# Read-out products moved into the last slots, a new tail order, outputs sent by quarters, and the last tile in column halves

## Chip, cores and metric

One core of one Trainium2 chip. The metric is the device time of one execution in microseconds (us), median of several runs. A profile's span, from first to last instruction, is about 1.8 us shorter than the time of the same run (210.28 against 212.04 for the kernel before).

## The reference, cut to what matters

```python
B, H, S, Ns, D = 8, 8, 512, 32, 64
xread = softmax(x @ state^T / 8) @ state           # per batch and head: 512 rows
sread = softmax(state @ x^T / 8) @ x               # 32 "read-out" rows
rows  = concat(xread, sread)                       # 8 batches of 544 rows of H*D = 512
out   = gelu(rows @ w_in) @ w_out                  # 512 -> 2048 -> 512, fp32 out: 4352 x 512
```

## The kernel before

Batches run one after another. In a batch, eight slots p = 0 to 7 each compute two 128-row blocks of the first layer (`M`, tile `hp`, GELU by ScalarE into `g`) beside one product of the second layer of the batch before. From the third batch on, the second layer is a seven-product (Strassen) scheme: products M1 to M7 of sums of quarters of `g` (`gsum`, VectorE) with sums of quarters of `w_out`; their results (`xp`, PSUM) are combined by adds into four quarters of the output. With rows in an upper and a lower half and columns in a left and a right one: M5 gives the upper right, M2 the lower left, M3, M6 and M1 the lower right, M1 and M7 the upper left. The 256 read-out rows of all batches go through the same scheme at the end (`R`, tiles `rp`, `osb`).

```python
def c22(b):                                     # after M2
    xs[b, "v"] = c_tile("v")
    nc.gpsimd.tensor_tensor(out=xs[b, "v"], in0=xs[b, "q"], in1=o[:, :, :NH], op=ALU.subtract)
    nc.vector.tensor_tensor(out=o[:, :, NH:], in0=xs[b, 3], in1=xs[b, "v"], op=ALU.add)
    x_out(b, 1)                                 # lower half of the rows, 512 KB
...
def X7_split(b):                                # last product of the last batch, two tiles
    for j in range(2):
        ps = xs[b, "x", j]
        x_mm(ps, xs[b, "g7"], w_sum["7"], False, (j,))
        nc.vector.tensor_tensor(out=o[:, j, :NH], in0=ps[:, 0, :], in1=xs[b, "u"][:, j, :], op=ALU.add)
        eng = nc.scalar if j else nc.sync
        eng.dma_start(out=rows[:, j, :NH], in_=o[:, j, :NH])     # 128 KB each
...
# the tail, after the last batch's slots
r_sums(); g_sum(b, "5"); X(b, "4"); g_sum(b, "1"); R("3"); R("4"); g_sum(b, "2"); X(b, "5")
nc.sync.dma_start(...)                          # upper right, 256 KB
R("5"); X1_split(b); g_sum(b, "7"); R("1"); X(b, "2"); R("2"); R("6"); R("7"); X7_split(b)
```

The softmax here doesn't subtract the row's maximum and nothing guards it: scores larger than these inputs give would overflow.

Of the kernel before, what the change touches and what calls it, by code (L numbers as in the profile page):

```python
# [12 lines left out]
ALU = mybir.AluOpType  # L13
# [4 lines left out]
def kernel(  # L18
# [8 lines left out]
    nc = tc.nc  # L27
# [471 lines left out]
    def mm2(b, q, j):  # L499
        if q == 0:  # L500
            ops[b, j] = otile([128, d_model], "op")
        ps = ops[b, j]
        for m in range(4 * q, 4 * q + 4):
            nc.tensor.matmul(  # L504
                ps,
                lhsT=gs[b][:, m, j * 128:(j + 1) * 128],
                rhs=w_out_bf[:, m, :],
                start=(m == 0),
                stop=(m == MC - 1),
            )  # L510
        if q == 3:
            rows = out_rows(b, j)
            h = d_model // 2 if j == SJ - 1 and b > 0 else d_model
            evac(ps, [(rows[:, n:n + h], slice(0, 128), n, n + h) for n in range(0, d_model, h)])

    def mm1_sr(m):
        hp = ps_f.tile([128, B * NS], FP32, name="hps", tag="f")
# [37 lines left out]
    def w_sums(i):  # L555
# [7 lines left out]
        )[i])  # L563

    xs = {}
    G_SUMS = {
        "1": ((0, 0), (1, 1), ALU.add),
        "2": ((1, 0), (1, 1), ALU.add),
# [26 lines left out]
    def c_tile(name):  # L595
        return cpool.tile([128, 2, NH], FP32, name=name, tag=name)

    def x_out(b, h):
        rows = out[b * SB:b * SB + S, :].rearrange("(p j) n -> p j n", j=SJ)
        nc.sync.dma_start(out=rows[:, 2 * h:2 * h + 2, :], in_=xs[b, "o", h])  # L600

    def c22(b):
        xs[b, "v"] = c_tile("v")
# [7 lines left out]
    def X(b, name):  # L611
        bank = {"3": 0, "4": 1, "5": 0, "2": 1, "1": 2, "6": 3, "7": 2}[name]
        first = name in "3416"
        if first:
            xs[b, bank] = otile([128, 2, NH], "xp", bank)
        ps = xs[b, bank]
        lhs = {"3": (0, 0), "4": (1, 1)}.get(name)
        lhs = xs[b, "g" + name] if lhs is None else g_q(b, *lhs)
        rhs = {"5": w_q[1][1], "2": w_q[0][0]}.get(name)
        rhs = w_sum[name] if rhs is None else rhs  # L620
        x_mm(ps, lhs, rhs, first)
        if name == "3":
            xs[b, "s3"] = c_tile("s3")
            nc.scalar.copy(out=xs[b, "s3"], in_=ps)
            for h in range(2):
                xs[b, "o", h] = hpool.tile([128, 2, d_model], FP32, name="oh", tag=f"oh{h}")
        elif name == "4":
            xs[b, "s34"] = c_tile("s34")
            nc.vector.tensor_tensor(out=xs[b, "s34"], in0=ps, in1=xs[b, "s3"], op=ALU.add)  # L629
        elif name == "5":  # L630
            o = xs[b, "o", 0][:, :, NH:]
            nc.scalar.copy(out=o, in_=ps)  # L632
            xs[b, "u"] = c_tile("u")
            nc.gpsimd.tensor_tensor(out=xs[b, "u"], in0=xs[b, "s34"], in1=o, op=ALU.subtract)  # L634
        elif name == "2":
            nc.scalar.copy(out=xs[b, "o", 1][:, :, :NH], in_=ps)  # L636
            c22(b)
        elif name == "1":
            xs[b, "q"] = c_tile("q")
            nc.vector.tensor_tensor(out=xs[b, "q"], in0=ps, in1=xs[b, "s34"], op=ALU.add)  # L640
        elif name == "7":
            nc.vector.tensor_tensor(
                out=xs[b, "o", 0][:, :, :NH], in0=ps, in1=xs[b, "u"], op=ALU.add
            )
            x_out(b, 0)

    def X1_split(b):
        xs[b, "q"] = c_tile("q")
        for j in range(2):
            ps = xs[b, "x", j] = otile([128, 1, NH], "xp", 2 - 2 * j)  # L650
            x_mm(ps, xs[b, "g1"], w_sum["1"], True, (j,))
            nc.vector.tensor_tensor(
                out=xs[b, "q"][:, j, :], in0=ps[:, 0, :], in1=xs[b, "s34"][:, j, :], op=ALU.add
            )

    def X7_split(b):
        rows = out[b * SB:b * SB + S, :].rearrange("(p j) n -> p j n", j=SJ)
        o = xs[b, "o", 0]
        for j in range(2):
            ps = xs[b, "x", j]  # L660
            x_mm(ps, xs[b, "g7"], w_sum["7"], False, (j,))
            nc.vector.tensor_tensor(
                out=o[:, j, :NH], in0=ps[:, 0, :], in1=xs[b, "u"][:, j, :], op=ALU.add
            )
            eng = nc.scalar if j else nc.sync
            eng.dma_start(out=rows[:, j, :NH], in_=o[:, j, :NH])

    rs = {}

    def r_q(h, k):  # L670
        return g_sr[:, MH * k:MH * k + MH, 128 * h:128 * h + 128]

    def r_sums():
        pair = [att.tile([128, 2, MH, 128], BF16, name="rs", tag="xT") for _ in range(2)]
        one = att.tile([128, MH, 128], BF16, name="rs1", tag="AT")
        homes = [pair[0][:, 0], pair[0][:, 1], pair[1][:, 0], pair[1][:, 1], one]
        for name, t in zip("51267", homes):
            (h0, k0), (h1, k1), op = G_SUMS[name]
            nc.vector.tensor_tensor(out=t, in0=r_q(h0, k0), in1=r_q(h1, k1), op=op)
            rs["g" + name] = t  # L680

    def r_out(h):
        nc.sync.dma_start(
# [4 lines left out]
    def R(name):  # L688
        def c_new(n):
            rs[n] = cpool.tile([128, NH], FP32, name="r_" + n, tag="r_" + n)  # L690
            return rs[n]

        bank = {"3": 0, "4": 1, "5": 0, "2": 1, "1": 2, "6": 3, "7": 2}[name]
        first = name in "3416"
        if first:
            rs[bank] = ftile([128, NH], "rp")
        ps = rs[bank]
        lhs = {"3": (0, 0), "4": (1, 1)}.get(name)
        lhs = rs["g" + name] if lhs is None else r_q(*lhs)
        rhs = {"5": w_q[1][1], "2": w_q[0][0]}.get(name)  # L700
        rhs = w_sum[name] if rhs is None else rhs
        for m in range(MH):
            nc.tensor.matmul(  # L703
                ps,
                lhsT=lhs[:, m, :],
                rhs=rhs[:, m, :],
                start=(first and m == 0),
                stop=(m == MH - 1),
                skip_group_check=True,
            )  # L710
        add, sub = ALU.add, ALU.subtract
        if name == "3":
            nc.scalar.copy(out=c_new("s3"), in_=ps)
            for h in range(2):
                rs["o", h] = opool.tile([128, d_model], FP32, name="osb", tag="osb")
        elif name == "4":
            nc.vector.tensor_tensor(out=c_new("s34"), in0=ps, in1=rs["s3"], op=add)
        elif name == "5":
            o = rs["o", 0][:, NH:]
            nc.scalar.copy(out=o, in_=ps)  # L720
            nc.gpsimd.tensor_tensor(out=c_new("u"), in0=rs["s34"], in1=o, op=sub)
        elif name == "1":
            nc.vector.tensor_tensor(out=c_new("q"), in0=ps, in1=rs["s34"], op=add)
        elif name == "2":
            o = rs["o", 1][:, :NH]
            nc.scalar.copy(out=o, in_=ps)
            nc.gpsimd.tensor_tensor(out=c_new("v"), in0=rs["q"], in1=o, op=sub)
        elif name == "6":
            nc.vector.tensor_tensor(out=rs["o", 1][:, NH:], in0=ps, in1=rs["v"], op=add)
            r_out(1)  # L730
        elif name == "7":
            nc.vector.tensor_tensor(out=rs["o", 0][:, :NH], in0=ps, in1=rs["u"], op=add)
            r_out(0)
# [126 lines left out]
    u = 17  # L860
# [24 lines left out]
    for b in range(2, B):  # L885
        nb = b + 1
        for p in range(8):
# [7 lines left out]
                xtr_dma(nb + 1)  # L895
            if p == 5 and nb < B:
                atr_dma(nb)
            if p == 3:
                srt(b)
            M(k, k + 1)  # L900
            if b == 2:
                for _ in range(2 if p < 4 else 1):
# [3 lines left out]
            elif p < 5:  # L906
# [2 lines left out]
                X(b - 1, "45127"[p])  # L909
                if p < 3:  # L910
                    g_sum(b - 1, "127"[p])
            if nb == B and 3 <= p < 7:
                for m in range(4 * p - 12, 4 * p - 8):
                    mm1_sr(m)
            if p == 1:
                sread(b)
                sread_out(b)
            if p == 0 and b + 3 < B:
                nc.gpsimd.tensor_copy(out=hold, in_=gs[b][:, 0, 0:1])  # L919
                load_x(b + 3)  # L920
# [2 lines left out]
                rearr(nb + 1)  # L923
            if p == 2 and nb + 1 < B:
                rearr_ones(nb + 1)
            if p == 5:
                g_sum(b, "6")
                if nb < B:
                    p_run(nb, (0, 1), ((0, 1), (3, 2)))
# [4 lines left out]
                    p_run(nb, (2, 3), ((1, 2), None))  # L934
                X(b, "6")
    b = B - 1
    r_sums()
    g_sum(b, "5")
    X(b, "4")
    g_sum(b, "1")  # L940
    R("3")
    R("4")
    g_sum(b, "2")
    X(b, "5")
    nc.sync.dma_start(
        out=out[b * SB:b * SB + S, :].rearrange("(p j) n -> p j n", j=SJ)[:, 0:2, NH:],
        in_=xs[b, "o", 0][:, :, NH:],
    )
    R("5")
    X1_split(b)  # L950
    g_sum(b, "7")
    R("1")
    X(b, "2")
    R("2")
    R("6")
    R("7")
    X7_split(b)


# [28 lines left out]
```

## Time and profile before

| | before |
|---|---|
| time, median (range), 4 runs | 212.66 us (212.36 to 212.92) |
| span of the profiled run | 210.28 us |
| PE busy | 200.7 us, 95% |
| first matmul of the second batch | 36.80 us |
| last matmul ends | 204.98 us |
| last output lands | 208.47 us |

### The profile page before, as it was taken

The page shows a single profiled execution, that of the slowest core. Times are in us where ns is not written, and L with a number is a line of the kernel's source. Part 1 is how long each engine was busy: PE and PEld are TensorE (multiplying, and loading weights), DVE is VectorE, ACT ScalarE, POOL GpSimd, SP SyncE. Part 2 cuts the span into 40 slices and gives each one's busy share as a digit, 9 for nine tenths or more (in the row PEclk, how much of TensorE's full clock was granted, in tenths as well). Part 3 has the DMA queues.
Part 4 walks back from the last instruction along what each step waited for, and adds up shares of the span by engine and source line. Part 5 has one row for each costly group of instructions (what it writes and reads, how often), then busy time and mean ns, then how long its engine had stood idle before and what let it go on. Part 6 is the DMA issues. An engine that isn't in the chain of part 4 may idle for free.

```text
span 210.3 us, 4666 instructions
## 1 busy us (share of the span) xinstructions
PE 200.7 (95%) x1955; PEld 130.9 (62%) x1963; DVE 134.5 (64%) x213; ACT 132.9 (63%) x240; POOL 65.9 (31%) x73
## 2 busy tenths in 40 slices
PE   7899999998999999999999999999999999999990
PEld 6645444453454577756775677567766777788880
DVE  1835675738829559984899558855885552357530
ACT  3864855679794779557956596678758455860110
POOL 8964301573270025700576007300220022000330
PEclk9999999999999999999999999999999999999997
DMA  6999999699275809355873910250016001300115
GB/s 200 187 172 204 206 194 193 141 203 174 45 100 124 228 0 128 76 199 54 113 90 131 193 29 3 86 165 3 2 58 194 3 0 59 143 0 0 53 64 187
DMA packets 37861, 23.14 MB, mean 110 GB/s; under 512 B 21712, under 2 KB 35280, under 8 KB 37840
## 3 DMA queue, kind: packets, MB, share of 16 engines
q0 software_dynamic: 13936, 8.10, 28.3%
q1 hardware_dynamic: 23216, 14.29, 27.2%
q10 hardware_dynamic: 688, 0.46, 0.7%
q8 instruction: 15, 0.25, 0.5%
q14 instruction: 6, 0.05, 0.1%
HBM read 17.30 MB, written 8.91 MB: 125 GB/s over the span
## 4 chain that ended last, share of the span: by engine, by line
PE 75%; DVE 11%; POOL 4%; DMA 3%; ACT 2%; issue 1%; POOLq 0%; DVEq 0%; ACTq 0%
PE xp L586 27%; PE hp L478 21%; PE op L504 9%; DVE gsum L580 5%; PE p_ps L415 4%; PE hps L519 3%; PE op L532 3%; DMA AT<-a 3%; PE rp L703 3%; DVE a L347 2%; POOL w_in_bf L105 2%; DVE cs L344 1%; PE sr L378 1%; PE pt L324 1%; POOL sbd L95 1%
## 5 line engine op out<-in xcount | busy, mean ns | idle before, releaser
L485 ACT ACTIVATE g<-hp 128x512 bf16<-128x512 f32 x124 | 67.6, 603 | 31.3 <-PE hp L478 26.0
L478 PE MATMUL hp<-AT,P 128*128 128x512 bf16 x248 | 64.2, 380 | 0.7 <-DVE XSR L405 0.4
L586 PEld LDWEIGHTS <-gsum 128*128 128x128 bf16 x480 | 46.5, 98 | 12.0 <-issue 2.1
L580 DVE TENSOR_TENSOR gsum<-g 128x2048 bf16<-128x2048 bf16 x30 | 39.4, 1327 | 0.0
L478 PEld LDWEIGHTS <-P 128*128 128x128 bf16 x248 | 22.1, 98 | 21.7 <-issue 4.0
L586 PE MATMUL xp<-ws,gsum 128*128 128x256 bf16 x288 | 34.4, 273 | 0.0
L427 DVE CAST P<-p_ps 128x512 bf16<-128x512 f32 x31 | 20.0, 683 | 18.1 <-PE p_ps L415 18.1
L634 POOL TENSOR_TENSOR u<-s,oh 128x512 f32<-128x512 f32 x6 | 7.6, 1266 | 66.8 <-ACT oh L632 66.8
L504 PE MATMUL op<-w_out_bf,g 128*128 128x512 bf16 x90 | 23.0, 379 | 0.3
L586 PE MATMUL xp<-ws,g 128*128 128x256 bf16 x192 | 22.9, 273 | 0.0
L586 PE MATMUL xp<-w_out_bf,gsum 128*128 128x256 bf16 x192 | 22.9, 273 | 0.0
L586 PEld LDWEIGHTS <-g 128*128 128x128 bf16 x192 | 18.8, 98 | 4.3
L426 ACT CAST P<-p_ps 128x512 bf16<-128x512 f32 x31 | 17.0, 604 | 6.8 <-PE p_ps L415 6.8
L218 POOL COPY x<-xb 128x1024 bf16<-128x1024 bf16 x12 | 12.6, 1081 | 11.7 <-DMA xb<-in_x_dram 11.7
L504 PEld LDWEIGHTS <-g 128*128 128x128 bf16 x96 | 9.1, 98 | 11.5 <-issue 1.1
L228 POOL COPY xo<-xb 128x1024 bf16<-128x1024 bf16 x12 | 14.5, 1240 | 1.3 <-PE sr L378 1.3
L347 DVE TENSOR_TENSOR a<-e,ics 128x512 bf16<-128x512 bf16 x14 | 13.9, 995 | 0.5
L605 POOL TENSOR_TENSOR v<-q,oh 128x512 f32<-128x512 f32 x6 | 7.6, 1274 | 15.1 <-ACT oh L636 15.1
L629 DVE TENSOR_TENSOR s<-xp,s 128x512 f32<-128x512 f32 x6 | 4.1, 692 | 12.8 <-PE xp L586 12.8
L415 PE MATMUL p_ps<-w_in_bf,sbd 64*32 64x512 bf16 x248 | 11.5, 382 | 0.8 <-ACT g L485 0.7
L344 DVE TENSOR_REDUCE cs<-e 128x16 f32<-128x512 bf16 x14 | 9.5, 676 | 3.8 <-ACT e L331 3.8
L919 POOL COPY hold<-g 128x1 bf16<-128x1 bf16 x3 | 1.0, 330 | 31.5 <-ACT g L485 31.5
(103 smaller groups left out, 214.9 us busy)
## 6 DMA issues: line engine op xcount, KB each, us to landing
out_dram<-oh SPq DMA_DIRECT2D x11, 512.0 KB, 2.9
xb<-in_x_dram POOLq DMA_DIRECT2D x7, 512.0 KB, 6.8
out_dram<-osb SPq DMA_DIRECT2D x9, 256.0 KB, 3.3
w_out_bf<-in_moe_w_out_dram POOLq DMA_DIRECT2D x4, 512.0 KB, 12.5
w_in_bf<-in_moe_w_in_dram POOLq DMA_DIRECT2D x6, 256.0 KB, 11.5
x0f<-in_x_dram SPq DMA_DIRECT2D x3, 256.0 KB, 4.1
w_in_bf<-in_moe_w_in_dram POOLq DMA_DIRECT2D x4, 128.0 KB, 4.3
x0f<-in_x_dram ACTq DMA_DIRECT2D x1, 256.0 KB, 4.6
```

The lines of the kernel that those rows point to most:

```text
L218: nc.gpsimd.tensor_copy(out=A.x4[:, :, :, 64 * t:64 * t + 64].rearrange("p j c d -> p c j d"), in_=src[:, t],)
L228: eng.tensor_copy(out=A.xo[:, :, :, 2 + 64 * t:66 + 64 * t].rearrange("p j c d -> p c j d"), in_=src[:, t],)
L344: nc.vector.reduce_sum(out=cs, in_=e4, axis=AX.X)
L347: nc.vector.tensor_tensor(out=A.a[:, :, hs].rearrange("p g (c n) -> p g c n", n=NS), in0=e4, in1=ics[:, :, :].to_broadcast((128, G, 2, NS) ...
L415: nc.tensor.matmul(ps[t][32 * c:32 * c + 32, :], lhsT=sbd[64 * t:64 * t + 64, b, c, 32 * t:32 * t + 32], rhs=w_in_bf[64 * t:64 * t + 64, c ...
L426: nc.scalar.copy(out=dst[:, 0, :], in_=ps[0])
L427: nc.vector.tensor_copy(out=dst[:, 1, :], in_=ps[1])
L478: nc.tensor.matmul(hp, lhsT=Ps[b][:, t, m * 128:(m + 1) * 128], rhs=atts[b].AT[:, :, t, :], start=(t == 0), stop=(t == 1),)
L485: nc.scalar.activation(out=gs[b][:, m, :], in_=hp, func=AF.Gelu)
L504: nc.tensor.matmul(ps, lhsT=gs[b][:, m, j * 128:(j + 1) * 128], rhs=w_out_bf[:, m, :], start=(m == 0), stop=(m == MC - 1),)
L580: nc.vector.tensor_tensor(out=t, in0=g_q(b, h0, k0), in1=g_q(b, h1, k1), op=op)
L586: nc.tensor.matmul(ps[:, j - js[0], :], lhsT=lhs[:, m, 128 * j:128 * j + 128], rhs=rhs[:, m, :], start=(first and j == js[0] and m == 0), ...
```

## The change

Its intent: let the read-out results leave earlier, so that the end has fewer outputs to drain; send each quarter when it is ready; make the last piece small. "48 transfers" counts the transfers issued by SyncE and ScalarE (42 before).

```diff
@@ mm2: first batches' outputs
-            h = d_model // 2 if j == SJ - 1 and b > 0 else d_model
-            evac(ps, [(rows[:, n:n + h], slice(0, 128), n, n + h) for n in range(0, d_model, h)])
+            evac(ps, [(rows, slice(0, 128), 0, d_model)])
@@ X: M5 and M7 of every batch but the last
+            x_out(b, 0, right)
...
-            x_out(b, 0)
+            x_out(b, 0, left)
@@ L1, L7: last batch (L4, L5, L5_u, L2 likewise; u and v on VectorE, no longer on GpSimd)
+        rows_out(1, both, right, nc.sync)
...
+        for j, pieces in ((0, ((0, NH),)), (1, ((0, h), (h, NH)))):
+            for n0, n1 in pieces:
+                # 8 matmuls into ps[:, 0, n0:n1], one VectorE add, one transfer
+                eng = nc.scalar if j and n0 else nc.sync
+                rows_out(0, slice(j, j + 1), slice(n0, n1), eng)
@@ last batch's attention read, one batch earlier (srt likewise, in slot 7)
+            if p == 4 and nb == B - 1:
+                sread(nb)
+                sread_out(nb)
@@ last batch's slots (nb == B)
-            if nb == B and 3 <= p < 7:
-                for m in range(4 * p - 12, 4 * p - 8):
+            if nb == B and p < 4:
+                for m in range(4 * p, 4 * p + 4):
                     mm1_sr(m)
+            if nb == B:
+                if p == 4:
+                    r_homes()
+                    r_sum("5")
+                    r_sum("2")
+                if p == 5:
+                    g_sum(b, "6")
+                    R("3")
+                    r_sum("1")
+                    R("4")
+                    r_sum("6")
+                    r_sum("7")
+                if p == 6:
+                    R("5")
+                    X(b, "3")
+                    R("2")
+                    R("1")
+                if p == 7:
+                    R("6")
+                    X(b, "6")
+                continue
@@ tail
-    (the order shown above)
+    for name in "521":
+        g_sum(b, name)
+    L4()
+    g_sum(b, "7")
+    L5()
+    L5_u()
+    L2()
+    R("7")
+    L1()
+    L7()
```

More of the change, by code (lines that the diff above doesn't have):

```diff
@@ L565 @@
     xs = {}
+    left, right = slice(0, NH), slice(NH, d_model)
     G_SUMS = {
@@ L596, in c_tile, with x_out @@
         return cpool.tile([128, 2, NH], FP32, name=name, tag=name)
-    def x_out(b, h):
+    def x_out(b, h, ns=slice(None)):
         rows = out[b * SB:b * SB + S, :].rearrange("(p j) n -> p j n", j=SJ)
-        nc.sync.dma_start(out=rows[:, 2 * h:2 * h + 2, :], in_=xs[b, "o", h])
+        nc.sync.dma_start(out=rows[:, 2 * h:2 * h + 2, ns], in_=xs[b, "o", h][:, :, ns])
     def c22(b):
@@ L644, in X, with rows_out, L4, L5 @@
             )
-            x_out(b, 0)
-    def X1_split(b):
-        xs[b, "q"] = c_tile("q")
+            x_out(b, 0, left)
+    def rows_out(h, js, ns, eng):
+        b = B - 1
+        rows = out[b * SB:b * SB + S, :].rearrange("(p j) n -> p j n", j=SJ)
+        eng.dma_start(
+            out=rows[:, 2 * h + js.start:2 * h + js.stop, ns], in_=xs[b, "o", h][:, js, ns]
+        )
+    both = slice(0, 2)
+    def L4():
+        b = B - 1
+        ps = xs[b, 1] = otile([128, 2, NH], "xp", 1)
+        x_mm(ps, g_q(b, 1, 1), w_sum["4"], True)
+        xs[b, "s34"] = c_tile("s34")
+        nc.vector.tensor_tensor(out=xs[b, "s34"], in0=ps, in1=xs[b, "s3"], op=ALU.add)
+        xs[b, "y"] = c_tile("q")
+        nc.vector.tensor_tensor(out=xs[b, "y"], in0=xs[b, 3], in1=xs[b, "s34"], op=ALU.add)
+    def L5():
+        b = B - 1
+        x_mm(xs[b, 0], xs[b, "g5"], w_q[1][1], False)
+        nc.scalar.copy(out=xs[b, "o", 0][:, :, right], in_=xs[b, 0])
+        rows_out(0, both, right, nc.sync)
+    def L5_u():
+        b = B - 1
+        xs[b, "u"] = c_tile("u")
+        nc.vector.tensor_tensor(
+            out=xs[b, "u"], in0=xs[b, "s34"], in1=xs[b, "o", 0][:, :, right], op=ALU.subtract
+        )
+    def L2():
+        b = B - 1
+        x_mm(xs[b, 1], xs[b, "g2"], w_q[0][0], False)
+        c21 = xs[b, "o", 1][:, :, left]
+        nc.scalar.copy(out=c21, in_=xs[b, 1])
+        rows_out(1, both, left, nc.sync)
+        xs[b, "v"] = c_tile("v")
+        nc.vector.tensor_tensor(out=xs[b, "v"], in0=xs[b, "y"], in1=c21, op=ALU.subtract)
+    def L1():
+        b = B - 1
         for j in range(2):
@@ L652, in X1_split, with L7 @@
             nc.vector.tensor_tensor(
-                out=xs[b, "q"][:, j, :], in0=ps[:, 0, :], in1=xs[b, "s34"][:, j, :], op=ALU.add
-            )
-    def X7_split(b):
-        rows = out[b * SB:b * SB + S, :].rearrange("(p j) n -> p j n", j=SJ)
+                out=xs[b, "o", 1][:, j, right],
+                in0=ps[:, 0, :],
+                in1=xs[b, "v"][:, j, :],
+                op=ALU.add,
+            )
+        rows_out(1, both, right, nc.sync)
+    def L7():
+        b = B - 1
         o = xs[b, "o", 0]
-        for j in range(2):
+        h = NH // 2
+        for j, pieces in ((0, ((0, NH),)), (1, ((0, h), (h, NH)))):
             ps = xs[b, "x", j]
-            x_mm(ps, xs[b, "g7"], w_sum["7"], False, (j,))
-            nc.vector.tensor_tensor(
-                out=o[:, j, :NH], in0=ps[:, 0, :], in1=xs[b, "u"][:, j, :], op=ALU.add
-            )
-            eng = nc.scalar if j else nc.sync
-            eng.dma_start(out=rows[:, j, :NH], in_=o[:, j, :NH])
+            for n0, n1 in pieces:
+                for m in range(MH):
+                    nc.tensor.matmul(
+                        ps[:, 0, n0:n1],
+                        lhsT=xs[b, "g7"][:, m, 128 * j:128 * j + 128],
+                        rhs=w_sum["7"][:, m, n0:n1],
+                        start=False,
+                        stop=(m == MH - 1),
+                        skip_group_check=True,
+                    )
+                nc.vector.tensor_tensor(
+                    out=o[:, j, n0:n1],
+                    in0=ps[:, 0, n0:n1],
+                    in1=xs[b, "u"][:, j, n0:n1],
+                    op=ALU.add,
+                )
+                eng = nc.scalar if j and n0 else nc.sync
+                rows_out(0, slice(j, j + 1), slice(n0, n1), eng)
     rs = {}
@@ L671, in r_q, with r_homes @@
         return g_sr[:, MH * k:MH * k + MH, 128 * h:128 * h + 128]
-    def r_sums():
+    def r_homes():
         pair = [att.tile([128, 2, MH, 128], BF16, name="rs", tag="xT") for _ in range(2)]
@@ L676, in r_sums, with r_sum @@
         homes = [pair[0][:, 0], pair[0][:, 1], pair[1][:, 0], pair[1][:, 1], one]
-        for name, t in zip("51267", homes):
-            (h0, k0), (h1, k1), op = G_SUMS[name]
-            nc.vector.tensor_tensor(out=t, in0=r_q(h0, k0), in1=r_q(h1, k1), op=op)
-            rs["g" + name] = t
+        rs["homes"] = dict(zip("51267", homes))
+    def r_sum(name):
+        t = rs["g" + name] = rs["homes"][name]
+        (h0, k0), (h1, k1), op = G_SUMS[name]
+        nc.vector.tensor_tensor(out=t, in0=r_q(h0, k0), in1=r_q(h1, k1), op=op)
     def r_out(h):
@@ L695, in R @@
         if first:
-            rs[bank] = ftile([128, NH], "rp")
+            home = {"3": 1, "4": 2, "6": 2}
+            rs[bank] = otile([128, NH], "rp", home[name]) if name in home else ftile([128, NH], "rp")
         ps = rs[bank]
@@ L720, in R @@
             nc.scalar.copy(out=o, in_=ps)
-            nc.gpsimd.tensor_tensor(out=c_new("u"), in0=rs["s34"], in1=o, op=sub)
+            nc.vector.tensor_tensor(out=c_new("u"), in0=rs["s34"], in1=o, op=sub)
         elif name == "1":
             nc.vector.tensor_tensor(out=c_new("q"), in0=ps, in1=rs["s34"], op=add)
+            nc.vector.tensor_tensor(
+                out=c_new("v"), in0=rs["q"], in1=rs["o", 1][:, :NH], op=sub
+            )
         elif name == "2":
@@ L726, in R @@
             nc.scalar.copy(out=o, in_=ps)
-            nc.gpsimd.tensor_tensor(out=c_new("v"), in0=rs["q"], in1=o, op=sub)
         elif name == "6":
@@ L897 @@
                 atr_dma(nb)
-            if p == 3:
+            if p == 3 and nb < B:
                 srt(b)
+            if p == 7 and nb == B - 1:
+                srt(nb)
             M(k, k + 1)
@@ L911 @@
                     g_sum(b - 1, "127"[p])
-            if nb == B and 3 <= p < 7:
-                for m in range(4 * p - 12, 4 * p - 8):
+            if nb == B and p < 4:
+                for m in range(4 * p, 4 * p + 4):
                     mm1_sr(m)
-            if p == 1:
+            if p == 1 and nb < B:
                 sread(b)
                 sread_out(b)
+            if p == 4 and nb == B - 1:
+                sread(nb)
+                sread_out(nb)
             if p == 0 and b + 3 < B:
@@ L936 @@
     b = B - 1
-    r_sums()
-    g_sum(b, "5")
-    X(b, "4")
-    g_sum(b, "1")
-    R("3")
-    R("4")
-    g_sum(b, "2")
-    X(b, "5")
-    nc.sync.dma_start(
-        out=out[b * SB:b * SB + S, :].rearrange("(p j) n -> p j n", j=SJ)[:, 0:2, NH:],
-        in_=xs[b, "o", 0][:, :, NH:],
-    )
-    R("5")
-    X1_split(b)
+    for name in "521":
+        g_sum(b, name)
+    L4()
     g_sum(b, "7")
-    R("1")
-    X(b, "2")
-    R("2")
-    R("6")
+    L5()
+    L5_u()
+    L2()
     R("7")
-    X7_split(b)
+    L1()
+    L7()
 _INS = ['x', 'state', 'moe_w_in', 'moe_w_out']
```

## The prediction

> **What bounds the kernel now.** I read the page first: PE is busy 95% of a 210.3 us span, the DMA engines are loaded mainly in the first half, and the granted clock is 0.994. So the body is limited by TensorE, and only two things can shorten the run: idle time on PE, or what follows PE's last matmul. I then asked for the busy time of each engine in stretches of the end. The columns are stretch, length, PE, PEld, DVE, ACT, POOL, granted clock, DMA busy share, GB/s.
>
> ```profile
> core 0: us, PE busy (x) PEld busy (x) DVE busy (x) ACT busy (x) POOL busy (x), PEclk, DMA share, GB/s
> 193.00:195.00 2.00, 2.00 (x21) 1.78 (x20) 2.00 (x3) 0.16 (x1) 0.00 (x0) 1.00 0.04 8
> 201.00:203.00 2.00, 2.00 (x21) 1.80 (x19) 0.35 (x1) 0.65 (x2) 1.65 (x2) 1.00 0.00 0
> 203.00:205.10 2.10, 1.98 (x19) 1.52 (x16) 1.60 (x5) 0.00 (x0) 0.30 (x1) 1.00 0.43 179
> ```
>
> All nine stretches from 187 to 205.1 look like this: 17.98 us of PE work in 18.1 us. The reader is to see that the tail has no PE gap. Moving the read-out products ("rp") earlier therefore cannot save PE time by itself; it only changes which results are late. What comes after PE's end (204.98) is 5.3 us, of which VectorE computes for 0.42:
>
> ```profile
> 203.00:204.00 1.00, 1.00 (x12) 0.90 (x10) 1.00 (x3) 0.00 (x0) 0.30 (x1) 1.00 0.00 0
> 204.00:205.00 1.00, 0.97 (x9) 0.62 (x7) 0.52 (x2) 0.00 (x0) 0.00 (x0) 1.00 0.78 324
> 205.00:206.00 1.00, 0.00 (x0) 0.00 (x0) 0.42 (x1) 0.00 (x0) 0.00 (x0) 1.00 1.01 297
> 206.00:207.00 1.00, 0.00 (x0) 0.00 (x0) 0.00 (x0) 0.00 (x0) 0.00 (x0) 1.00 0.98 344
> 207.00:208.00 1.00, 0.00 (x0) 0.00 (x0) 0.00 (x0) 0.00 (x0) 0.00 (x0) 0.88 0.96 342
> 208.00:209.00 1.00, 0.00 (x0) 0.00 (x0) 0.00 (x0) 0.00 (x0) 0.00 (x0) 0.50 0.01 4
> ```
>
> From 204.2 to 208.0 the DMA engines are full. The timeline of the same stretch says with what:
>
> ```profile
> 202.65 0.69 DVE L608 TENSOR_TENSOR oh<-xp,v 128x512 f32<-128x512 f32 x1 [2.73 <-POOL v L605]
> 203.40 0.33 SPq L600 DMA_DIRECT2D out_dram<-oh  x1
> 203.84 1.31 SPq L683 DMA_DIRECT2D out_dram<-osb  x2
> 204.14 0.42 DVE L662 TENSOR_TENSOR oh<-xp,u 128x256 f32<-128x256 f32 x1
> 205.01 0.42 DVE L662 TENSOR_TENSOR oh<-xp,u 128x256 f32<-128x256 f32 x1 [0.45 <-PE xp L586]
> 205.24 0.54 SPq L666 DMA_DIRECT2D out_dram<-oh  x1
> 205.47 0.37 ACTq L666 DMA_DIRECT2D out_dram<-oh  x1
> ```
>
> 512 KB (L600), 2 x 128 KB (L683) and 2 x 128 KB (L666): 1 MB issued between 203.40 and 205.47, because the half L600 waits for POOL's v and DVE, and the read-out sums come right behind. The last transfer is issued at 205.47 and lands 3.0 us later, 208.47; the span ends 1.8 us after that. The two rows of issues and landings below show that most of the 3.0 us is a queue: twice the bytes, sent alone at 196.06, took 2.1 us.
>
> ```profile
> out_dram<-oh SPq DMA_DIRECT2D x1, 256.0 KB, 2.1
> out_dram<-oh ACTq DMA_DIRECT2D x1, 128.0 KB, 3.0
> ```
>
> For that lone transfer the stretches show DMA busy from about 197.0 to 197.75: some 0.9 us from issue to first packet, 0.75 us for 256 KB, 0.4 us to the landing. I use these three numbers below.
>
> **What the Trainium skill says.** (1) "DMA: Bandwidth & Descriptors", section "Anatomy of one DMA — SWDGE (gpsimd) path", gives a fixed cost of about 2.0 us per DMA, mostly completion. The lone 256 KB took 2.1 us in all, so here the fixed part is nearer 1.3 us; I use the trace. (2) The same page, "Issuing engines are not separate DMA queues": transfers from SP and ACT share the same engines. The trace agrees: the 128 KB issued by ACT waits behind SP's. (3) "PSUM — Partial Sum Buffer", "PSUM bank collisions raise a hardware error": TensorE and VectorE may not touch one bank and quadrant together, even in different columns, so software orders them. No gap in the kernel before shows it, as its two last tiles lie in two banks; in the changed program the first matmul of the second column half carries a wait on VectorE, and its count is that of the add of the first half. (4) "VectorE: DVE Perf Modes" gives (N+151)/0.96 ns for an fp32 tensor-tensor add. The trace agrees: 424 ns at 256, 690 at 512; at 128 it makes 291 ns.
>
> **The change part by part.**
>
> *Same PE work, new order.* The matmuls are the same, except that the last tile's 8 of 256 columns (L586, 109 ns apart: 16 in 1.91 us) become 16 of 128. Eight 128-column transposes at full clock took 0.61 us, and one takes 0.22, so the spacing is (0.61-0.22)/7 = 56 ns: 16 x 56 = 0.90 against 8 x 109 = 0.87 us. Cost: 0.03 us.
>
> *Read-out work in the last slots.* The read-out's 64 first-layer matmuls move three slots earlier (the last batch's attention read moves into the batch before, to feed them), and six of the seven products go into the last batch's slots 5 to 7 (of 0 to 7). A slot here is 1.0 us (hp) + 1.8 + 1.8 on PE against 1.1 + 1.6 + 0.6 on ACT at most, as it was. Walking the new order with these durations, I put the last batch's M4 at 195.2, M5 at 197.0, M2 at 198.7, R7 at 200.5, M1 at 201.35, M7's first tile at 203.1. Each operand I checked is there: the first read-out sum at 185.3 for a product at 187.4, the GELU at 193.6 for a VectorE sum needed at 197.0. No stall, 0 us.
>
> *VectorE in the tail.* From 193.7 it must do one 0.42, three sums of 1.22, s34 and y 0.69 each, a sum 1.22, u and v 0.69 each, and three adds of 0.42: 9.3 us before 204. In order: s34 ends 198.46 (its bank is wanted by M2 at 198.73), M5's u about 201.0, M2's v 201.95, R7's add 202.37, M1's adds 202.84 and 203.69 (wanted by M7 at 203.1 and 203.97). Three margins of 0.26 to 0.28 us, none negative. POOL's 1.27 us v and u and their waits leave the path.
>
> *The split last tile.* First half: matmuls 203.97 to 204.59 (8 x 56 + 0.17 us of latency). VectorE add 204.62 to 204.91. The second half must wait for it (point 3): 204.96 to 205.58. Add to 205.90, issue from ACT at 205.94. Before it was 205.47, so the last issue comes **0.47 us later**: 0.29 for the add between, 0.17 for the second latency, 0.08 for the two handovers, 0.03 for the spacing, less the 0.13 by which the last add is shorter (0.44, and 0.03 of rounding).
>
> *The outputs.* M5's and M2's 256 KB each are issued at about 199.5 and 201.3 and gone before 203.3. Of the 1 MB, what is left behind PE's end is: R7's 128 KB at 202.4, M1's 256 KB at 203.75, 128 KB at 204.6, 64 KB at about 205.1 and 64 KB at 205.94. Packets of M1's run from 204.65 to 205.4, of the 128 KB from 205.5 to 205.9, of the first 64 KB from 206.0 to 206.2. When the last one's packets start, at 205.94 + 0.9 = 206.84, the engines are free; 0.2 us of data and 0.4 to landing make **207.45**, where before it was 208.47. Saved: **1.0 us**, net of the later issue.
>
> *Quarters in the earlier batches.* Five 512 KB outputs become two of 256 KB each, one of them three slots earlier, ahead of the transposes that feed the next batch. PE waits for those transposes 0.2 us in the whole run. Somewhere between 0 and -0.2 us; I take 0. The split of the first batches' last tile is dropped: nothing.
>
> Sum: 212.6 - 1.0 = **211.6 us**.
>
> **The rivals.** *A: VectorE becomes the bound of the tail.* For it: 9.3 us of work in 10.3 us and margins under 0.3 us; a g sum averages 1.33 us over the run and 1.21 to 1.22 in the tail, where POOL is still. Against it: POOL has nothing left in the new tail. If VectorE slips by 0.5 us, PE stalls by what exceeds the margin and the time is about 212.0. *B: the wait between the column halves is longer* than 0.4 us (semaphore and pipeline refill), or the SP queue, at 0.35 to 0.65 us an issue, holds up M1's transfer; then half the gain goes: 212.1. *C: the last slots stall PE* because read-out tiles take the banks of the main stream (homes 1 and 2, and one of the four rotating banks held by R1 until R7). Three such waits of 0.4 us would eat the gain: 212.7. *D: the body gains too*, because the output traffic no longer stands before the transposes, and the landing is quicker than 1.5 us: 211.1. The order shows where the waits are but no durations, so C is the one I can least exclude.
>
> **Range and chances.** Centre 211.6; A to C pull up by 0.4 to 1.1, D down by 0.5, and the three runs before already differ by 0.56. Range 210.9 to 212.5. Two percent is 4.25 us; there are only 5.3 us after PE's end and 1.8 of them are fixed, so faster by 2% is nearly excluded, and slower needs a stall that I see nowhere.
>
> **What would show it.** Right: DMA share near full for less than 2 us after PE's end, with a gap before the last transfer; the last landing about 1.5 us after its issue; a PE idle of 0.3 to 0.45 us put down to the VectorE add between the two halves; no other PE wait after 185. Wrong: PE waiting for s34, v or M1's adds (A); a landing still near 3 us (the queue is not relieved); hp or rp waiting on ACT or DVE in slots 4 to 7 (C).

## The result, and the profile after

The median is 210.76 us (210.25 to 211.33, 4 runs) against 212.66; the ratio is 0.9912 (0.9883 to 0.9941). A ratio here is the mean time of one kernel's fast runs over that of the other's of the same rounds, so it is not quite the ratio of the medians. The time fell by 1.9 us where 1.0 was forecast, and lies 0.14 us below the range.

First the tail, as in the prediction. The timeline of the changed kernel (start, duration, engine, line, operation, idle before it and what ended it):

```profile
199.55 2.12 SPq L651 DMA_DIRECT2D out_dram<-oh  x2
201.30 0.69 DVE L686 TENSOR_TENSOR v<-q,oh 128x512 f32<-128x512 f32 x1 [0.58 <-ACT oh L683]
202.36 0.56 SPq L743 DMA_DIRECT2D out_dram<-osb  x1
203.26 0.42 DVE L693 TENSOR_TENSOR oh<-xp,v 128x256 f32<-128x256 f32 x1 [0.45 <-PE xp L586]
203.71 1.74 SPq L651 DMA_DIRECT2D out_dram<-oh  x3
204.93 0.61 PE L709 MATMUL xp<-ws,gsum 128*128 128x128 bf16 x8 [0.38 <-DVE oh L717]
205.57 0.29 DVE L717 TENSOR_TENSOR oh<-xp,u 128x128 f32<-128x128 f32 x1 [0.70 <-PE xp L709]
205.89 0.37 ACTq L651 DMA_DIRECT2D out_dram<-oh  x1
```

v ends at 201.99 (forecast 201.95), M1's second add at 203.68 (203.69), the second column half starts at 204.93 (204.96) after the forecast wait of 0.38 us on VectorE, and the last transfer is issued at 205.89 (205.94). The stretches of the end (columns as in the prediction):

```profile
203.00:204.00 1.00, 1.00 (x13) 0.90 (x11) 0.42 (x1) 0.00 (x0) 0.00 (x0) 1.00 0.39 88
204.00:205.00 1.00, 0.62 (x11) 0.50 (x10) 0.72 (x2) 0.00 (x0) 0.00 (x0) 1.00 0.76 254
205.00:206.00 1.00, 0.53 (x8) 0.36 (x7) 0.29 (x1) 0.00 (x0) 0.00 (x0) 1.00 0.91 318
206.00:207.00 1.00, 0.00 (x0) 0.00 (x0) 0.00 (x0) 0.00 (x0) 0.00 (x0) 1.00 0.40 120
207.00:208.00 1.00, 0.00 (x0) 0.00 (x0) 0.00 (x0) 0.00 (x0) 0.00 (x0) 1.00 0.03 7
```

The DMA engines are full only until 206.3 and then idle until the last 64 KB, which now lands on its own latency:

```profile
out_dram<-oh SPq DMA_DIRECT2D x1, 128.0 KB, 1.9
out_dram<-oh SPq DMA_DIRECT2D x1, 64.0 KB, 1.7
out_dram<-oh ACTq DMA_DIRECT2D x1, 64.0 KB, 1.6
```

It lands at 207.53, forecast 207.45. So far the prediction holds, though the agreement to 0.1 us in absolute times is partly luck: this run started 0.43 us later than the other and gained nearly as much in its body, as will be seen. But the span ends at 208.46, only 0.93 us after that landing; in the kernel before it was 1.81. And the body changed: on PE, one wait is gone. The timeline of PE near 120 us in the kernel before, then in the changed kernel:

```profile
119.24 0.93 PE L586 MATMUL xp<-ws,gsum 128*128 128x256 bf16 x7
120.36 1.04 PE L478 MATMUL hp<-AT,P 128*128 128x512 bf16 x4 [0.19 <-DMA AT<-a]
121.24 0.93 PE L586 MATMUL xp<-ws,g 128*128 128x256 bf16 x7
```

```profile
119.23 1.36 PE L586 MATMUL xp<-ws,gsum 128*128 128x256 bf16 x11
120.43 1.03 PE L478 MATMUL hp<-AT,P 128*128 128x512 bf16 x4
121.30 0.93 PE L586 MATMUL xp<-ws,g 128*128 128x256 bf16 x7
```

The batch that ends there took 22.19 us and not 22.54 (first `hp` matmul to first `hp` matmul). The parts of the run, from the two profiles:

| us | before | after | difference |
|---|---|---|---|
| second batch's start to last matmul's end | 168.17 | 168.30 | +0.13 |
| last matmul's end to last landing | 3.49 | 2.00 | -1.49 |
| last landing to end | 1.81 | 0.93 | -0.88 |
| sum | 173.47 | 171.22 | -2.25 |

(The two profiled spans differ by 1.82 only, as the start-up of the changed kernel's run happened to take 0.43 longer.)

What is in the 0.88? The page of instructions does not show waits of SyncE, but a view of the end marker's line does; in stretches that begin just after the last landing, kernel before, then the changed one (engine, operation, count, durations in ns, first and last start):

```profile
L983 SPq EVENT_SEMAPHORE  x9: 17/28/28, 208.5 to 210.2; - x9
L983 SPq DRAIN  x3: 7/7/13, 209.4 to 209.7; - x3
```

```profile
L1061 SPq EVENT_SEMAPHORE  x3: 17/17/28, 207.5 to 208.4; - x3
L1061 SPq DRAIN  x3: 7/7/13, 207.6 to 207.9; - x3
```

Nine against three. The single starts, read from the same traces, in the order in which SyncE checks the semaphores of the transfers (transfers take the eight semaphores in turn, and the last of all is marked *):

```
check      1st     2nd      3rd     4th     5th     6th     7th     8th      drain   end
before   208.26  208.48*  208.55  208.64  208.72  209.20  209.29  209.36    209.43  210.28
after    205.55  205.62   205.68  205.75  206.20  206.54  206.75  207.54*   207.61  208.46
```

In the kernel before, the 42nd transfer counts on the second semaphore: SyncE passes it at 208.48 and still has six checks to do, with a pause of 0.48 us among them, 0.95 us until the drain. With 48 transfers the last one counts on the eighth, and SyncE has done the other seven while the transfer was under way: 0.07 us until the drain. (The step before its fifth check, at 206.20, is no pause but a wait: that semaphore's transfer landed at 206.18. Where the pause went is told after e5.) From the drain on, both take 0.85 us.

### The profile page after: what moved, and what is told of

Read it like the earlier page. It is cut to its first block, busy times and chain, and to the rows that moved or that the text cites. A ratio compares the mean times of both kernels' runs of the same rounds, so it can differ in the third digit from the quotient of the medians.

```text
span 208.5 us, 4699 instructions
## 1 busy us (share of the span) xinstructions
PE 201.5 (97%) x1971; PEld 131.6 (63%) x1971; DVE 137.5 (66%) x218; ACT 133.2 (64%) x240; POOL 62.4 (30%) x69
## 4 chain that ended last, share of the span: by engine, by line
PE 78%; DVE 12%; POOL 4%; ACT 3%; issue 1%; POOLq 0%; DVEq 0%; ACTq 0%
PE xp L586 28%; PE hp L478 22%; PE op L504 9%; DVE gsum L580 5%; PE p_ps L415 4%; PE op L531 3%; PE hps L518 3%; PE rp L764 3%; DVE a L347 2%; POOL w_in_bf L105 2%; DVE cs L344 1%; PE sr L378 1%; PE pt L324 1%; POOL sbd L95 1%; ACT g L870 1%
## 5 line engine op out<-in xcount | busy, mean ns | idle before, releaser
L586 PEld LDWEIGHTS <-gsum 128*128 128x128 bf16 x464 | 45.0, 98 | 11.5 <-issue 2.1
L586 PE MATMUL xp<-ws,gsum 128*128 128x256 bf16 x272 | 32.5, 273 | 0.0
L504 PE MATMUL op<-w_out_bf,g 128*128 128x512 bf16 x96 | 23.7, 379 | 0.0
L635 POOL TENSOR_TENSOR u<-s,oh 128x512 f32<-128x512 f32 x5 | 6.3, 1268 | 49.0 <-ACT oh L632 49.0
L605 POOL TENSOR_TENSOR v<-q,oh 128x512 f32<-128x512 f32 x5 | 6.4, 1279 | 14.8 <-ACT oh L637 14.8
L629 DVE TENSOR_TENSOR s<-xp,s 128x512 f32<-128x512 f32 x5 | 3.5, 692 | 11.0 <-PE xp L586 11.0
```

The lines of the kernel that those rows point to most:

```text
L504: nc.tensor.matmul(ps, lhsT=gs[b][:, m, j * 128:(j + 1) * 128], rhs=w_out_bf[:, m, :], start=(m == 0), stop=(m == MC - 1),)
L586: nc.tensor.matmul(ps[:, j - js[0], :], lhsT=lhs[:, m, 128 * j:128 * j + 128], rhs=rhs[:, m, :], start=(first and j == js[0] and m == 0), ...
```

## The experiments

Each run was profiled and timed against the kernel before on its chip. "To PE's end" counts from the second batch's start, as in the table above.

| run | to PE's end | to landing | to end | time, median | ratio (95%) |
|---|---|---|---|---|---|
| before | 168.17 | 3.49 | 1.81 | 212.66 | |
| changed | 168.30 | 2.00 | 0.93 | 210.76 | 0.9912 (0.9883 to 0.9941) |
| e1 before, 48 transfers | 168.24 | 4.20 | 0.93 | 212.35 | 0.9972 (0.9947 to 0.9998) |
| e2 changed, 50 transfers | 168.30 | 1.99 | 1.29 | 210.57 | 0.9906 (0.9875 to 0.9936) |
| e3 before, M2 quarter early | 168.25 | 3.30 | 1.71 | 211.95 | 0.9961 (0.9934 to 0.9988) |
| e4 both, on before | 168.28 | 3.88 | 0.93 | 212.61 | 0.9987 (0.9957 to 1.0017) |
| e5 before, 56 transfers | 169.37 | 3.54 | 0.93 | 212.13 | 0.9978 (0.9957 to 0.9999) |
| e6 changed, batches' halves whole | 168.76 | 1.99 | 0.91 | 211.43 | 0.9945 (0.9915 to 0.9974) |
| e7 changed, last tile whole | 167.74 | 2.35 | 0.92 | 209.66 | 0.9862 (0.9840 to 0.9884) |
| e8 changed, halves in two banks | 167.79 | 2.02 | 0.91 | 209.83 | 0.9869 (0.9845 to 0.9893) |
| e9 changed, upper read-out late | 168.31 | 2.68 | 0.91 | 211.66 | 0.9959 (0.9909 to 1.0008) |
| e10 e9's edit and M2 quarter late | 168.31 | 2.00 | 0.93 | 210.31 | 0.9893 (0.9850 to 0.9937) |
| e11 changed again | 168.30 | 2.00 | 0.91 | 209.60 | 0.9882 (0.9830 to 0.9935) |

Theory S said that SyncE's walk through the eight semaphores is the 0.88 us; theory Q that the rest is the queue of output transfers. Their rivals: the end is a fixed cost, and the order of the computing pays.

**e1.** Six early outputs are cut in two, nothing else.

```diff
-            h = d_model // 2 if j == SJ - 1 and b > 0 else d_model
+            h = d_model // 2 if (b, j) in ((0,0),(0,1),(0,2),(0,3),(1,0),(1,1),(1,3)) else d_model
```

> The kernel before, with six early 256 KB outputs cut into two, so that it issues 48 hardware transfers and not 42, and the last one to issue counts on the last of the eight semaphores that SyncE checks at the end. Theory S (the end is SyncE's walk through the eight semaphores, and a last transfer on the second of them leaves six checks, 0.95 us, after the landing): last landing unchanged near 208.5, span 209.4 (0.9 us less), time 211.75. Rival (the end is a fixed cost, or 0.9 us of the gain came from the tail's transfers): span unchanged at 210.3, time 212.6.

From landing to end: 0.93, exactly as S says. But the landing came 0.7 us later than before, which S had not foreseen, and ate most of it. Two things had moved. SyncE's pause now fell before its last issue: the second-last transfer was issued 0.74 us after PE's end, not 0.27. In the timeline ScalarE's issue now stands ahead of it:

```profile
205.75 0.37 ACTq L666 DMA_DIRECT2D out_dram<-oh  x1
205.99 0.34 SPq L666 DMA_DIRECT2D out_dram<-oh  x1
```

And a transfer of kind "instruction" (8 KB on one engine, 0.68 us) stands among the last outputs; the view of DMA in the stretch 207 to 208 has it:

```profile
q14 instruction: 1, 0.01, 4.3%
```

In the trace the last output's sixteen engines had finished by 208.60 but for one, which came at 209.45. The fifteen are 3.35 us behind PE's end, no later than in the kernel before, so the loss is that one engine's 0.85 us. In the kernel before, this fetch came at 209.8, after everything; in the changed kernel at 203.0, 2.5 us before PE's end.

**e2.** The changed kernel with two early outputs cut in two: 50 transfers.

> The changed kernel with two early outputs cut in two: 50 transfers, the last on the second semaphore again. Theory S: last landing unchanged near 207.5, then six more checks, some 0.4 to 0.9 us more to the end (0.4 if the pause of 0.48 us seen between the fifth and sixth check comes at another place): span 208.9 to 209.4, time 211.2 to 211.7. Rival (fixed end): span 208.5, time 210.8.

To the landing 1.99, from there to the end 1.29: six further checks at 62 ns, 0.37 us, with no pause among them. S holds, at its lower size. The time shows nothing of 0.37 us.

**e3.** The kernel before, with one transfer split.

```diff
             nc.scalar.copy(out=xs[b, "o", 1][:, :, :NH], in_=ps)
+            if b == B - 1:
+                x_out(b, 1, slice(0, NH))
             c22(b)                      # its x_out then sends the right half alone for the last batch
```

> The kernel before, with only the last batch's left half of the lower rows (the M2 quarter, 256 KB, ready when ScalarE has copied it) sent as soon as it is ready; everything else in the old order; 43 transfers, the last on the third semaphore. Theory Q (the queue of output transfers behind the last matmul set the last landing, not where the read-out products stand): last landing 207.3 and not 208.5, span about 209.1, time 211.5. Rival (moving the read-out products and the adds off GpSimd is what pays): last landing and time as before, 212.6, or less than 0.3 us below.

The landing came 3.30 us after PE's end, 0.2 earlier, not 1.2. So Q as I had put it, that this quarter is what matters, is wrong. One reason is a size: the lines of issues for that stretch of the kernel before give the read-out outputs as 256 KB each, where I had used 128.

```profile
out_dram<-oh SPq DMA_DIRECT2D x1, 512.0 KB, 2.6
out_dram<-osb SPq DMA_DIRECT2D x2, 256.0 KB, 3.3
```

The queue of the kernel before was 1.28 MB, and with the quarter out of it 1.02 MB remain, issued late, the first read-out output among them being slow (its first 64 packets of 2 KB took 148 ns each on average, later ones about 90; in the kernel before 160 and about 90). From the landing to the end, 43 transfers leave five checks and the pause: 1.71 us, as S would have it.

**e4.** e3 and five early outputs cut in two.

> Both: the early M2 quarter and five early outputs cut in two, 48 transfers, last one on the last semaphore; read-out products and tail order as in the kernel before. If the two effects S and Q are all of the gain: span 208.3, time 210.6, as the changed kernel or 0.2 us below it. If moving the products or the column halves is worth something by itself: 211 or more.

It missed: 0.93 to the end as S says, but 3.88 to the landing, and a time no better than before. The instruction fetch fell at 208.6, among the last outputs, and the last one finished on fifteen engines by 209.79 and on the sixteenth at 210.55. Even the fifteen came 3.12 us after PE's end, where the changed kernel needs 2.00. So S and Q without the rest of the change do not make its gain.

**e5.** As e1, with the early outputs cut into up to four (14 transfers more), so that the fetch falls ahead of the end.

> The kernel before with 14 more early transfers (56 in all, last one again on the last semaphore), so that SyncE's late instruction fetch of 8 KB, which fell among the last outputs in the two 48-transfer runs and held one of the 16 DMA engines for 0.68 us, falls ahead of them. Theory S with the fetch as the disturber: from PE's end to the last landing 3.5 us as in the kernel before (4.2 and 3.9 in the disturbed runs), from landing to end 0.93, and the issue of the second-last transfer no longer 0.48 us late: 0.9 us gained, time 211.8. Rival (more transfers of themselves delay the landing): 4.2 us again, time 212.4.

The fetch came at 183.6, and the way to the landing is back at 3.54 with 0.93 to the end. The two kernels e1 and e5 differ only in how early outputs are cut. So the late landing in e1 goes with the fetch, not with the number of transfers. That the late engine is the one that carried the fetch is inferred: the trace does not name engines, but in e1, e4, e6 and e9 the sixteenth engine falls 0.28 to 0.85 us behind the fifteenth in transfers that land just after the fetch, against 0.14 us at most in the tails of the other runs. The walk's gain of 0.88 us is there. The body, however, is 1.20 us longer, as the many small early outputs brought a new PE wait, so that by its parts the profiled run is 0.37 us longer than the kernel before, while the median time is 0.5 us shorter. The profiled run (212.93) was the slowest of six, the others 211.99 to 212.32; that they did not have this wait is likely, but not shown.

```profile
56.77 1.04 PE L478 MATMUL hp<-AT,P 128*128 128x512 bf16 x4 [1.00 <-DMA AT<-a]
```

*Where the pause lies.* The kept traces settle what e1 and e5 leave half open. Number SyncE's recorded instructions from 0. In the six runs where nothing else holds SyncE at that point (the kernel before, e1, e2, e3, e4, e9), a pause of 0.45 to 0.46 us stands right before number 79, whatever that instruction is; in e1 it is the second-last output's issue. In the other seven runs SyncE stands still there for 0.47 us or more, as it waits for an engine. In the changed kernel, which has 13 more instructions on SyncE (100 against 87), number 79 is the issue of R7's output at 202.36, where SyncE waits 0.62 us for VectorE. So the pause belongs to SyncE's instruction stream, and adding instructions moves it off the end. Of the 0.88 us, the six checks are 0.37 (e2 has them back, without the pause), and the rest, about 0.5, is mostly the pause's new place.

**e6.** The changed kernel, with the two `x_out` calls of the middle batches merged again and five early outputs cut in two.

> The changed kernel with the five batches' outputs sent in whole halves again (512 KB), and five early outputs cut in two so that there are still 48 transfers. If the quarters keep output traffic away from the transposed load that feeds the next batch: the PE gap of about 0.2 us near 120 us returns and PE's end is 0.2 to 0.35 us later from the second batch's start (168.5 to 168.65 and not 168.30); tail as in the changed kernel (2.0 us to the landing, 0.93 us to the end). Rival (the quarters do nothing): 168.30.

The wait returned, and PE's end is 0.46 us later, more than expected; the tail is unchanged.

```profile
121.57 0.61 PE L478 MATMUL hp<-AT,P 128*128 128x512 bf16 x2 [0.28 <-DMA AT<-a]
```

**e7.** The last tile in one piece, one early output cut in two (48 transfers).

```diff
-        for j, pieces in ((0, ((0, NH),)), (1, ((0, h), (h, NH)))):
+        for j, pieces in ((0, ((0, NH),)), (1, ((0, NH),))):
```

> The changed kernel with the last tile not cut in column halves (one 128 KB transfer; one early output cut in two, 48 transfers). By the sums of the prediction the halves cost 0.47 us of PE and issue time and save 0.2 us of data: PE's end 0.5 us earlier, from PE's end to the landing 2.2 us and not 2.0, so last landing about 0.3 us earlier, time 210.4 against 210.7. Rival (the halves pay): landing later than 0.5 us from PE's end plus 2.0.

PE's end came 0.56 us earlier and the landing 0.35 later from there: 0.22 us gained by the profile (expected 0.3), and the ratio of times, 0.9862, is below the changed kernel's 0.9912 and 0.9882 (e11), but on another chip and with intervals that overlap. By the profile the column halves in one bank cost more than they save.

**e8.** The halves in two banks: M1's second tile too is computed in two halves.

```diff
+    LAST = ((0, 0, NH, 2), (1, 0, NH // 2, 0), (1, NH // 2, NH, 3))   # tile, columns, bank
```

> The changed kernel with the last tile's column halves in two PSUM banks (M1's second tile computed in two halves too), so that PE need not wait for VectorE between them. No PE gap of 0.38 us at the end, PE's end 0.45 us earlier, landing 1.9 to 2.0 us after it: 0.45 us less than the changed kernel, time 210.3. Rival: VectorE's one more add (0.29 us) makes M7 wait and eats it.

No PE wait at the end; the landing, 2.02 us after PE's end, is 0.50 us earlier from the second batch's start than in the changed kernel (169.80 against 170.30; expected 0.45), and the rival's wait for VectorE is not there. By the profile e7 and e8 beat both kernels (171.00 and 170.72 us from the second batch's start to the end, against 171.22 and 173.47); their times, 209.66 and 209.83, cannot be told apart, while by the profile e8 ends 0.28 us earlier.

**e9, e10, e11.** The upper read-out output is issued after R7; in e10 the M2 quarter also waits and goes with M1's.

> The changed kernel, but the upper read-out output (256 KB, ready 8 us earlier) is held back and sent just before the lower one, after R7. Compute as in the changed kernel. By the transfer sums (256 KB in 0.75 us, the first read-out transfer slower, 1.2 us) the queue then ends near 206.8 where the last transfer's first packet was at 206.75: landing 0.1 to 0.2 us later, 2.1 to 2.2 us after PE's end. If the read-out's move pays mainly through this transfer: 0.5 us or more later. If it pays through compute: no change.

> As the run before, and the M2 quarter is held back too and sent with M1's as one 512 KB transfer (one early output cut in two, 48 transfers): the tail's output queue is as long as in the kernel before (1.28 MB), all compute as in the changed kernel. Queue theory: the engines are busy until about 207.7, landing 0.6 us later than in the changed kernel (2.6 us after PE's end), time 0.6 us more. If compute order made the landing early: 2.0 us as in the changed kernel.

> The changed kernel itself, as the reference for the two runs before it on the same chip: PE's end to landing 2.0 us, landing to end 0.93 us, 168.3 us from the second batch's start to PE's end; time 0.990 to 0.993 of the kernel before.

e9's landing is 0.68 us later, but not for the reason given. Fifteen of the last transfer's engines had finished by 208.79, 2.12 us after PE's end, as the transfer sum said; the sixteenth came at 209.35. The fetch, at 205.4 here, fell among the outputs again; it took 0.31 us itself, less than the 0.56 us by which the sixteenth engine was late. e10 did not do what its expectation supposes: with the M2 issue out of the way, SyncE could issue the upper read-out output right after M5's, at 200.2, so only the M2 quarter was late. Its landing is the same 2.00 us. So the M2 quarter's early sending is worth nothing here; the last transfer's own latency hides it.

## Why the prediction was wrong, step by step

- **No PE gap, so no PE time from moving products: right.** VectorE's three margins held and no `rp` or `hp` waited at the end (rivals A and C did not occur).
- **The split last tile costs 0.47 us of issue time: right.** From the second batch's start, the changed kernel issues its last transfer 0.43 us later than e7 does, which differs from it by the split and one early output cut in two (168.66 against 168.23). PE waits 0.38 us between the halves, and e8 removes that.
- **The outputs: right in the sum, wrong in a term.** "2 x 128 KB (L683)" and "R7's 128 KB" should read 256 KB each. It did not matter to the last landing, as the queue was empty again at 206.3, before the last transfer's first packet. It did matter to my reading of e3.
- **"Somewhere between 0 and -0.2 us; I take 0": mis-sized.** The quarters in the middle batches measured -0.35 us between the two kernels and -0.46 in e6. The wait shows as 0.19 and 0.28 us of idle PE; I had taken that for its whole size. But in the traces a 256-column matmul lasts 0.27 us while the next starts 0.11 us after it, so a PE that runs idle also loses 0.16 us of overlap: 0.35 and 0.44 us, which is what the batch lost (22.54 and, in e6, 22.63 us against 22.19). This is the first half of rival D. (The table's first row is +0.13 us because the split moved PE's end by 0.56 us the other way, by e7; 0.08 us are left over and not accounted for.)
- **"There are only 5.3 us after PE's end and 1.8 of them are fixed": the failed step.** Of the 1.8, 0.95 were SyncE's walk with its pause; 48 transfers put the last one on the last semaphore and left 0.07. That is -0.88 us (e1, e4 and e5 show it in the kernel before, e2 in the changed one in reverse).

Added up: -1.0 for the tail as forecast, -0.35 and -0.88 give -2.2 us; the parts show -2.25. The measured times (ratio 0.9912, and 0.9882 in e11, so 1.9 and 2.5 us) lie on both sides of it.

What stays open: that the 8 KB fetch is SyncE's own. The trace does not name its reader; the fetch begins 0.6 to 1.4 us after SyncE's instruction 79 in the six runs where the pause is seen, and it moved with SyncE's instruction count from e1 to e5. How much of the landing's 1.49 us is owed to the read-out output leaving early and how much to its being out of the fetch's way was not separated cleanly: e9 has 0.1 us of the one and 0.6 of the other.

## What to carry to other kernels

Measure what follows the last landing, not only what comes before it: here 0.9 us lay in the order in which one engine checks eight semaphores and in a pause of that engine, and the number of transfers moved both. Splitting the last tile paid here only with its halves in different PSUM banks. To size a PE wait, add to the idle time that the profile shows the overlap that is lost with it. A change in the number of instructions moves instruction fetches too, and one that falls among the last outputs can take back as much as the change had won.

## What the Trainium skill lacked or had wrong

- No page gives the cost of the checks at the end: six checks left after the last landing took 0.37 us (62 ns each, e2), or 0.95 us with a pause of 0.48 us among them (kernel before). Nor does a page have that pause, 0.45 us before SyncE's recorded instruction 79.
- No page gives what an instruction fetch costs an output beside it; it would belong to "DMA: Bandwidth & Descriptors". Fetches of 8 KB took 0.68, 0.65 and 0.31 us, and the last output's part on one engine landed 0.85, 0.75 and 0.56 us after the other fifteen (e1, e4, e9).
- The same page fits its fixed cost of about 2.0 us to transfers issued from GpSimd, and has no such fit for those issued by SyncE and ScalarE: here a 64 KB output issued by ScalarE took 1.6 us in all.
- "TensorE: Matmul & The Clock Gate", section "Back-to-back issue gap", gives about 81 ns between pairs of weight load and 128-column matmul in a sustained stream, and about 56 ns without the weight loads; here runs of 8 (changed kernel) and 16 (e8) such pairs kept 56 ns with them. No longer run of them was measured.
